# Constants put into the planned order, two output buffers for three, and ten DMA transposes with unused results, in a strided attention and FFN kernel

## Chip, core and metric

The kernel runs on one core of a Trainium2 chip. The metric is the device time of one execution in microseconds (us); the time before is the median of four runs.

## What is computed

The reference takes q, k and v of 8 batches, 8 heads, 576 positions and 64 elements, and five float32 matrices. Heads 0 to 3 attend to the last 32 positions ("local"), heads 4 to 7 to earlier positions with the same remainder modulo 32 ("strided"). The attention output, as 4,608 rows of 512, goes through a multiplicative feed-forward network (FFN):

```
scores = scale * q @ k^T
mask_local   = (rel >= 0) & (rel < 32)
mask_strided = (rel >= 0) & (pos_k % 32 == pos_q % 32)
attn = softmax(where(mask, scores, -1e9)) @ v
x = attn as (4608, 512)
out = ((x @ w1) * (x @ w2)) @ w3 @ w_out
```

## The kernel before, in words

**Stages.** The kernel multiplies w3 and w_out once into one matrix (w34): eight blocks of w3 are transposed on TensorE (`tr`, L552), evicted, and multiplied with w_out (`mm`, L571). Beside that, batch by batch, it does the attention of four pairs of heads (hp 0 and 1 local, 2 and 3 strided): q and k are transposed on TensorE (`T`, L643; the last 64 positions of all heads in one go, `R`, L596), scores (`S`, L686; for batch 0 with a mask bias added by matmuls, L677), exps on ACT (L704), the mask product on DVE (L712), the product with v (`X`, L724 and L734), and the division by the sum, on ACT and DVE (L763 to L790) or on DVE and with a transpose back (L752, L753, `U`, L803). The result is xT, fp16. As soon as the batches of a tile of 512 tokens are done, the FFN of that tile runs, nine tiles in all: for each of eight column blocks jc a product `a` with w1 (L838), its copy asb on ACT, a product `b` with w2 (L854) and the product of both on DVE (L860); then four outputs `o` (L874) of 128 rows each, copied to osb on ACT (L304) and stored by SyncE (L893). A name such as o2_3 is tile 2, output 3; T4_2 is batch 4, pair of heads 2.

**Loads and casts.** All inputs are float32. SyncE loads them through seven staging buffers (`stg`), in the order of the list `_loads`, and POOL casts each to fp16 (L308): q and k of four heads a time (`x16`, two buffers a name), the last positions (`x16r`), v (`v16L`, `v16S`, two buffers by parity of the batch; the columns beyond the 64 elements hold ones, so that the product with v also gives the sums), and the weights.

**What sets the order.** Every step is an operation of a planner (`Plan`): its engines with costs in ns, what it waits for, what it takes and gives back (four PSUM banks "f", two double banks "B", the staging buffers, two asb, three osb, and others), and a rank. `Plan.order` walks through time with those costs and with a rough model of DMA, and picks for each engine the ready operation of lowest rank. It starts each engine at a fixed time (L95: DVE at 6500, ACT at 3200, POOL at 4200), since the constants that stand ahead of the plan occupy it until then. Where TensorE has nothing to do in the first 26 us it inserts a filler matmul (`ps_spin`, L328), which works on zeros. The operations are then issued in the planned order, and each engine executes its own queue strictly in that order. SyncE's queue holds loads and stores alike: a store that waits for its copy, or a load that waits for a staging buffer, holds up all that stands behind it. DMA completions are counted on eight semaphores in rotation, so that a DMA also waits for the one eight before it.

**The constants** stand ahead of the plan (L324 to L387) and are only pinned in part: on POOL the identity, the local mask, `sel` and the causal mask; on DVE zeros for the fillers' weights, kTS, kTL and `place` (L324 to L363), two copies of the identity into `place` (L364, L365), the ones and zeros of v16L and v16S (L382 to L386), the products maskK and maskS and two biases (L373 to L380); on ACT `idR` (L342) and copies of the ones to the second buffers (L385, L387). TensorE makes the strided mask with two small matmuls (L371), which stand at the head of its queue. In the built program DVE does the v16 fills before the two copies into `place`.

**The osb ring.** A copy into osb waits until the store of the copy that used the buffer before has landed.

Of the kernel before, what the change touches and what calls it, by code (L numbers as in the profile page):

```python
# [9 lines left out]
FP32 = mybir.dt.float32  # L10
# [40 lines left out]
class Plan:  # L51
# [34 lines left out]
    def order(self, slack=0, start=None, spin=None, first=("ACT", "DVE", "POOL")):  # L86
# [5 lines left out]
            for d in o.deps:  # L92
                d.succ.append(o)
        free = {k: [(0, i) for i in range(n)] for k, n in self.cap.items()}
        busy = dict(SP=800, POOL=4200, ACT=3200, DVE=6500, PE=1500)  # L95
        busy.update(start or {})
        avail = {e: [] for e in busy}
        for o in ops:
# [158 lines left out]
def kernel(  # L257
# [11 lines left out]
    nc = tc.nc  # L269
# [24 lines left out]

    NSTG = cfg.get("nstg", 8)
    stgs = [consts.tile([P, DF], FP32, name=f"st{i}") for i in range(NSTG)]
    plan = Plan(dict(f=NF, B=2, stg=NSTG, asb=2, osb=3, rcp=2, xqs=2, w3n=3, abt=4))

    def pin(ins):
        return tc.keep_in_program_order(ins)  # L300
# [20 lines left out]

    pin(nc.scalar.preload_act_table_set("natural_log_exp_and_others"))
    w34 = consts.tile([P, KF, DM], FP16)
    nc.vector.memset(w34[:, 0, :], 0.0)  # L324

    def spin(key):
        ps = bank("f", key, [P, DM], FP32)
# [5 lines left out]
    v16L = [consts.tile([P, 4, LT, P], FP16, name=f"v16L{i}") for i in range(2)]  # L333
    v16S = [consts.tile([KB, 4, ST, P], FP16, name=f"v16S{i}") for i in range(2)]
    ptms = [consts.tile([P, 576], FP16, name=f"ptm{i}") for i in range(4)]
    nc.vector.memset(kTS, 0.0)
    nc.vector.memset(kTL[:, :, 0:32], 0.0)
    id16 = consts.tile([P, P], FP16)
    make_identity(nc, id16)

    idR = consts.tile([P, NR], FP16)
    nc.scalar.copy(out=idR.rearrange("p (g u t) -> p g u t", g=4, u=2),  # L342
                   in_=id16[:, 32:32 + NR].rearrange("p (t u g) -> p g u t", u=2, g=4))

    maskL = consts.tile([P, LQ], FP16)
    nc.gpsimd.memset(maskL, 1.0)
# [13 lines left out]
    nc.gpsimd.affine_select(out=causal, in_=causal, compare_op=ALU.is_ge, fill=0.0, base=0,  # L360
                            pattern=[[1, SQ]], channel_multiplier=-1)
    place = consts.tile([SQ, KB], FP16)
    nc.vector.memset(place, 0.0)  # L363
    nc.vector.tensor_copy(out=place[0:64, 32:KB], in_=id16[0:64, 0:64])  # L364
    nc.vector.tensor_copy(out=place[64:SQ, 0:32].rearrange("k (i f) -> k f i", f=4)[:, 0], in_=id16[64:SQ, 64:SQ])  # L365
    maskK = consts.tile([SQ, SQ], FP16)
    maskS = consts.tile([KB, SQ], FP16)
    sel2 = sel.rearrange("r a b -> r (a b)")
    for i, (lhs, rhs, n) in enumerate(((sel2, sel2, SQ), (place, maskK, KB))):
        mps = psp.tile([P, 512], FP32, tag=f"f{i}", name="mps")  # L370
        pin(nc.tensor.matmul(mps[0:n, 0:SQ], lhs, rhs, start=True, stop=True))  # L371
        if i == 0:
            nc.vector.tensor_mul(maskK, mps[0:n, 0:SQ], causal)  # L373
        else:
            nc.vector.tensor_copy(out=maskS, in_=mps[0:n, 0:SQ])

    biasL = consts.tile([P, LQ], FP16)
    biasS = consts.tile([KB, SQ], FP16)
    for o, i in ((biasL, maskL), (biasS, maskS)):
        nc.vector.tensor_scalar(out=o, in0=i, scalar1=-1.0, scalar2=30000.0, op0=ALU.add, op1=ALU.mult)  # L380

    nc.vector.memset(v16L[0][:, :, :, D:P], 1.0)  # L382
    nc.vector.memset(v16L[0][0:32, :, 0, :], 0.0)
    nc.vector.memset(v16S[0][:, :, :, D:P], 1.0)  # L384
    nc.scalar.copy(out=v16L[1][:, :, :, D:P], in_=v16L[0][:, :, :, D:P])  # L385
    nc.vector.memset(v16L[1][0:32, :, 0, 0:D], 0.0)  # L386
    nc.scalar.copy(out=v16S[1][:, :, :, D:P], in_=v16S[0][:, :, :, D:P])  # L387

    xT = [consts.tile([P, NTOK], FP16, name=f"xT{cc}") for cc in range(4)]
    w1h = consts.tile([P, KM, DF], FP16)  # L390
    w2h = consts.tile([P, KM, DF], FP16)
# [20 lines left out]
        o.clean = clean if first else 0  # L412
        return o

    early = []

    def cast(name, key, dmas, eng, fn, deps=(), take=(), last=True, rank=10):
        if eng == POOL and len(early) < cfg.get("early", 0):
            eng = {"POOL": 1040, "DVE": 700, "ACT": 1048}
            early.append(key)  # L420
        return plan.op(name, eng, fn, deps=list(dmas) + list(deps), take=take,
                       give=[("stg", key)] if last else [], rank=rank, lock=True)

    CE = cfg.get("cast", {})
# [38 lines left out]
    def load_qk(b, grp):  # L463
        for nm, ten in (("q", q), ("k", k)):
            key = f"{nm}{b}_{grp}"
            d = dma(key, key, 1530, [P, 4, 4, D],
                    lambda s: s.rearrange("p h c d -> p h (c d)"),
                    ten[b, 4 * grp:4 * grp + 4, 0:NM].rearrange("h (p c) d -> p h (c d)", c=4))

            def fn(e, nm=nm, key=key):  # L470
                t = qkp.tile([P, 4, 4, D], FP16, tag=f"{nm}{grp}", name="x16")
                copy(e, t, stg[key].rearrange("p h c d -> p c h d"))
                x16[(b, nm, grp)] = t

            c = cast("c" + key, key, [d], CE.get("qk", POOL), fn)
            x16op[(b, nm, grp)] = c
            late.append((c, lambda: [Top.get((b - 2, h)) for h in (2 * grp, 2 * grp + 1)]))

    def load_rest(b):
# [19 lines left out]
    def load_vL(b, hp):  # L499
        vt = v16L[b % 2]  # L500
        hs = slice(2 * hp, 2 * hp + 2)
        key = f"vL{b}_{hp}"
        ds = []
        ds.append(dma(key, key, 1500, [P, 2, LT, D], lambda s: s[32:P].rearrange("p h t d -> p (h t) d"),
                      _ap(v, (b * H + 2 * hp) * S * D, [[D, LQ], [LQ * D, 2 * LT], [1, D]]), clean=0))
        cs = []
        for i, pr in enumerate((bass.ds(32, 32), bass.ds(64, 64))):
            def fn(e, pr=pr):
                copy(e, vt[pr, hs, :, 0:D], stg[key][pr])
            c = cast(f"c{key}{i}", key, ds, {"POOL": 825}, fn, last=(i == 1))  # L510
            late.append((c, lambda: [PVop.get((b - 2, h, g)) for h in (0, 1) for g in (0, 1)]))
            cs.append(c)
        hl = plan.op(f"h{key}", cfg.get("halo", {"POOL": 660}),
                     lambda e: copy(e, vt[0:32, hs, 1:LT, 0:D], vt[96:P, hs, 0:LT - 1, 0:D]),
                     deps=cs, rank=9, lock=True)
        late.append((hl, lambda: [PVop.get((b - 2, h, g)) for h in (0, 1) for g in (0, 1)]))
        for g in range(2):
            vop[(b, hp, g)] = cs + [hl]
# [71 lines left out]
    for b in range(B):  # L590
# [28 lines left out]
        for pi, hp in enumerate(cfg["pord"](b)):  # L619
# [51 lines left out]
            def fnS(e, hp=hp, nm2=nm2, w=w, m=m, kT=kT, kw=kw, local=local, pm=pm):  # L671
# [8 lines left out]
                for g in range(2):  # L680
                    sps = bank("B", f"S{nm2}_{g}")
                    for i in range(m):
                        ks, qs = kw * (g * m + i), w * (g * m + i)
                        for h in range(2):
# [2 lines left out]
                                                 qT[r_, hp, qs:qs + w], start=not pm, stop=not pm or i == m - 1))  # L687

            s = Sop[(b, hp)] = plan.op(f"S{nm2}", {"PE": (300 if local else 360) + 500 * pm}, fnS,
                                       deps=evs + Rev + prevPV, take=[("B", f"S{nm2}_0"), ("B", f"S{nm2}_1")],  # L690
                                       rank=rank("S"), soft=True, mode=1)
            for g in range(2):
                sk = f"S{nm2}_{g}"
# [43 lines left out]

                if old:
                    fp = fpo
                pv = PVop[(b, hp, g)] = plan.op(pk, {"PE": 246}, fp, deps=[mo] + vop[(b, hp, g)],  # L740
                                                take=[("B", pk)], rank=rank(f"P{g}"), soft=True)
                ptmu[pslot] = pv
                newPV[g] = pv
# [78 lines left out]
    for t in range(NTILE):  # L822
# [41 lines left out]
        for ts in range(NT // P):  # L864
            parts = 2 if (t == NTILE - 1 and ts == NT // P - 1) else 1
            nw = DM // parts
            for pt in range(parts):
                key = f"o{t}_{ts}_{pt}"
                h = None
                for hf in range(2):  # L870
                    def fo(e, t=t, ts=ts, hf=hf, key=key, pt=pt, nw=nw):
                        ps = bank("f", key, [P, nw], FP32) if hf == 0 else bank("f", key)
                        for ci in range(4 * hf, 4 * hf + 4):
                            pin(nc.tensor.matmul(ps, big[("abt", t)][:, ci, bass.ds(ts * P, P)],  # L874
                                                 w34[:, ci, bass.ds(pt * nw, nw)], start=(ci == 0),
                                                 stop=(ci == KF - 1)))

                    h = plan.op(f"o{t}_{ts}_{pt}_{hf}", {"PE": 864 // parts}, fo,
                                deps=[muls[4 * hf + i] for i in range(4)] + w34op[8 * hf:8 * hf + 8] + [h],
                                take=[("f", key)] if hf == 0 else [], rank=100 + 24 * t + 17 + 2 * ts + 0.001 * hf,  # L880
                                give=[("abt", f"abt{t}")] if ts == 3 and hf == 1 and pt == parts - 1 else [])

                def fc(e, key=key, nw=nw):
                    osb = ffn.tile([P, nw], FP32, tag="osb", bufs=3, name="osb")
                    live[("osb", key)] = osb
                    copy(e, osb, bank("f", key))

                oe = {"ACT": 590 // parts + 60, "DVE": 690 // parts} if parts > 1 else cfg.get("osb", {"ACT": 590})
                c = plan.op(f"osb{key}", oe, fc, deps=[h], take=[("osb", key)], give=[("f", key)], rank=4)

                def fd(e, key=key, t=t, ts=ts, pt=pt, nw=nw):
                    eng = nc.scalar if e == "ACT" else nc.sync
                    pin(eng.dma_start(out_r[t * (NT // P) + ts][:, bass.ds(pt * nw, nw)], live[("osb", key)]))  # L893

                plan.op(f"st{key}", cfg.get("st", {"SP": 450}), fd, deps=[c],
                        give=[("osb", key)], rank=4.5, dma=750 // parts, store=True)
# [42 lines left out]
```

The softmax here doesn't subtract the row's maximum and nothing guards it: scores larger than these inputs give would overflow.

## Time and profile before

| | us |
|---|---|
| runs before | 280.34, 280.70, 281.23, 281.30; median 280.97 |
| the profiled execution's own time | 280.09 |
| span in the profile, first to last instruction | 278.4 |
| PE (TensorE) busy | 266.7 |
| DVE, ACT busy | 174.1, 173.8 |
| POOL busy | 117.9, none of it after 179 us |

The profile counts the time from the first instruction. PE is TensorE's matmuls, PEld its weight loads, SP is SyncE. Bytes moved are 48.65 MB, of them 38.80 MB read from HBM and 9.44 MB written. The granted TensorE clock is 1.0 throughout. In the views a row of the timeline gives start and length in us, engine, line, operation, output<-input, shape and count; in brackets the idle time before it and what ended that.

### The profile page before, as it was taken

The numbers are of one execution on the slowest core, as the hardware profiler recorded it, in microseconds if no ns is written. First come the engines' busy times: TensorE is split into PE (matmuls) and PEld (weight loads), VectorE is DVE, ScalarE is ACT, GpSimd is POOL, SyncE is SP. The second block draws the span as 40 slices with busy tenths as digits, with TensorE's granted clock in tenths as the row PEclk, the third lists the DMA queues.
The fourth block names the chain that finished last, engine by engine and source line by source line (L and its number), as shares of the span: only waits on it lengthen the run. The fifth ranks groups of instructions, "written<-read, shape, count | busy, mean of one in ns | idle before, by whom it ended". The sixth has DMA issues, their size and how long they took to land.

```text
span 278.4 us, 6299 instructions
## 1 busy us (share of the span) xinstructions
PE 266.7 (96%) x2434; PEld 150.8 (54%) x2434; DVE 174.1 (63%) x328; ACT 173.8 (62%) x321; POOL 117.9 (42%) x146
## 2 busy tenths in 40 slices
PE   0989999999999999999999999999999999999995
PEld 0468895746555555555555555555555544444443
DVE  7254677777578667866785778577857763320321
ACT  3562587856667866776588658866885775324321
POOL 6676997599969969450735083100000000000000
PEclk9999999999999999999999999999999999999999
DMA  7999999999999999978365300210030003003004
GB/s 255 322 353 268 355 356 359 259 270 316 298 290 283 338 269 305 264 215 251 105 171 191 122 1 2 114 40 2 1 114 39 2 11 142 1 0 151 2 0 151
DMA packets 53422, 48.65 MB, mean 175 GB/s; under 512 B 20752, under 2 KB 45584, under 8 KB 53392
## 3 DMA queue, kind: packets, MB, share of 16 engines
q1 hardware_dynamic: 53392, 48.24, 57.6%
q8 instruction: 19, 0.31, 0.5%
q14 instruction: 11, 0.09, 0.1%
HBM read 38.80 MB, written 9.44 MB: 173 GB/s over the span
## 4 chain that ended last, share of the span: by engine, by line
PE 95%; DVE 4%; issue 0%; ACT 0%; DVEq 0%
PE ps_o L874 23%; PE ps_b L854 22%; PE ps_a L838 22%; PE ps_T L643 5%; PE ps_mm L571 5%; PE ps_S L686 4%; PE ps_X L734 3%; PE ps_X L724 3%; PE ps_spin L328 2%; PE ps_U L803 2%; PE ps_tr L552 1%; DVE v16S L384 1%; PE ps_R L596 1%; PE ps_S L677 1%; DVE xqs L753 0%; DVE v16L L382 0%
## 5 line engine op out<-in xcount | busy, mean ns | idle before, releaser
L860 DVE TENSOR_TENSOR abt<-ps_b,asb 128x512 f16<-128x512 f32 x72 | 49.4, 689 | 39.3 <-PE ps_b L854 38.7
L838 PE MATMUL ps_a<-xT,w1h 128*128 128x512 f16 x288 | 73.8, 379 | 0.0
L854 PE MATMUL ps_b<-xT,w2h 128*128 128x512 f16 x288 | 73.8, 379 | 0.0
L874 PE MATMUL ps_o<-w,abt 128*128 128x512 f16 (+1 forms) x296 | 67.4, 374 | 0.0
L304 ACT COPY asb<-ps_a 128x512 f32<-128x512 f32 x72 | 42.2, 588 | 40.3 <-PE ps_a L838 39.4
L308 POOL CAST x<-st 128x1024 f16<-128x1024 f32 x32 | 32.7, 1036 | 32.3 <-PE ps_T L643 20.0
L854 PEld LDWEIGHTS <-w2h 128*128 128x128 f16 x288 | 26.9, 98 | 29.2
L874 PEld LDWEIGHTS <-abt 128*128 128x128 f16 x296 | 26.9, 98 | 27.7
L838 PEld LDWEIGHTS <-w1h 128*128 128x128 f16 x288 | 26.5, 98 | 26.6
L704 ACT ACTIVATE ps_S<-ps_S 96x576 f32<-96x576 f32 (+1 forms) x56 | 32.9, 628 | 11.0 <-PE ps_S L686 10.5
L304 ACT COPY osb<-ps_o 128x512 f32<-128x512 f32 x35 | 20.5, 587 | 18.5 <-PE ps_o L874 18.2
L790 DVE TENSOR_TENSOR xT<-ps_X,rcp 64x288 f16<-64x288 f32 x56 | 25.1, 448 | 5.6 <-ACT rcp L774 5.0
L308 POOL CAST v16L<-st 32x768 f16<-32x768 f32 (+1 forms) x32 | 26.3, 821 | 3.1 <-DMA st<-in_v_dram 1.1
L712 DVE TENSOR_TENSOR ptm<-ps_S,maskL 128x576 f16<-128x576 f32 x28 | 19.8, 750 | 12.0 <-ACT ps_S L704 12.0
L753 DVE TENSOR_TENSOR xqs<-ps_X,rcq 96x384 f16<-96x384 f32 (+1 forms) x36 | 20.5, 569 | 1.2
L712 DVE TENSOR_TENSOR ptm<-ps_S,maskS 96x576 f16<-96x576 f32 x28 | 19.8, 749 | 1.3 <-ACT ps_S L704 0.5
L643 PE MATMUL ps_T<-id,x 128*128 128x128 f16 x256 | 19.1, 219 | 0.0
L308 POOL CAST v16S<-st 96x1024 f16<-96x1024 f32 x16 | 16.4, 1033 | 6.3 <-PE ps_X L724 6.3
L774 ACT ACTIVATE rcp<-ps_X 64x576 f32<-64x576 f32 x28 | 18.1, 647 | 0.9
L763 ACT ACTIVATE ps_X<-ps_X 64x576 f32<-64x576 f32 x28 | 17.7, 632 | 0.9 <-PE ps_X L724 0.5
L306 DVE COPY qT<-ps_T 128x512 f16<-128x512 f16 x16 | 11.1, 692 | 9.6 <-PE ps_T L643 8.3
L734 PEld LDWEIGHTS <-ptm 128*96 128x96 f16 (+1 forms) x224 | 14.2, 123 | 4.3
(80 smaller groups left out, 277.0 us busy)
## 6 DMA issues: line engine op xcount, KB each, us to landing
out_dram<-osb SPq DMA_DIRECT2D x35, 256.0 KB
st<-in_moe_w_dram SPq DMA_DIRECT2D x16, 512.0 KB
st<-in_q_dram SPq DMA_DIRECT2D x16, 512.0 KB
st<-in_k_dram SPq DMA_DIRECT2D x16, 512.0 KB
st<-in_v_dram SPq DMA_DIRECT2D x16, 288.0 KB
st<-in_v_dram SPq DMA_DIRECT2D x16, 256.0 KB
st<-in_moe_w_out_dram SPq DMA_DIRECT2D x4, 512.0 KB
st<-in_q_dram SPq DMA_DIRECT2D x8, 128.0 KB
```

Source lines behind the costliest of these rows:

```text
L304: pin(nc.scalar.copy(out=out, in_=in_))
L308: pin(nc.gpsimd.tensor_copy(out=out, in_=in_))
L643: pin(nc.tensor.transpose(ps[:, c * P:(c + 1) * P], x16[(b, x, hp // 2)][:, c, h0:h0 + 2] .rearrange("p h d -> p (h d)"), id16))
L704: pin(nc.scalar.activation(out=sps, in_=sps, func=AF.Exp, bias=0.0, scale=scale))
L712: pin(nc.vector.tensor_mul(ptm[0:kr, 0:576].rearrange("p (h a x) -> p h a x", h=2, x=w), pte[0:kr].rearrange("p h (a x) -> p h a x", x=w), ...
L734: pin(nc.tensor.matmul(xps[0:w, h, i * 65:(i + 1) * 65], ptms[pslot][0:kr, c0:c0 + w], vt[0:kr, 2 * (hp % 2) + h, g * m + i, 0:D + 1], sta ...
L753: pin(nc.vector.tensor_mul(xqs[0:w, 0:m].rearrange("p i h d -> p h i d"), xv[:, :, :, 0:D], _ap(rcp, 0, [[rcp.ap[0][0], w], [4, 2], [1, m] ...
L790: pin(nc.vector.tensor_mul(o, i0, i1))
L838: pin(nc.tensor.matmul(ps, w1h[:, ci, js], xT[ci][:, tok], start=(ci == 0), stop=(ci == KM - 1)))
L854: pin(nc.tensor.matmul(ps, w2h[:, ci, js], xT[ci][:, tok], start=(ci == 0), stop=(ci == KM - 1)))
L860: pin(nc.vector.tensor_mul(big[("abt", t)][:, jc, :], bank("f", f"b{t}_{jc}"), live[("asb", t, jc)]))
L874: pin(nc.tensor.matmul(ps, big[("abt", t)][:, ci, bass.ds(ts * P, P)], w34[:, ci, bass.ds(pt * nw, nw)], start=(ci == 0), stop=(ci == KF - ...
```

## The change

1. **Constants in the plan.** The fills, copies, masks and biases become operations of the planner, pinned in its order. The planner's start times become POOL 3000, ACT 2150, DVE 1300. DVE now does kTS, kTL, `place` and the copies into `place` first, then the masks and biases, then the fills of v16S and v16L; ACT does `idR` first, and the copies of the ones after. The two mask matmuls are planned too: four fillers stand ahead of the first one in TensorE's queue, one between them. A product with v waits for its ones, a score with bias for the biases.
2. **osb has two buffers, not three.** This gives room for 2 KB a partition of a new tile, `junk`. As the planner is told so, it moves output copies back: in tiles 1 to 3 the copies of outputs 2 and 3 stand behind asb copies of the next tile. From tile 1 on TensorE's order changes in places: for example b2_7 stands behind the scores S3_3, and o2_0's second half behind the first half of o2_1.
3. **Ten DMA transposes.** For batches 3 to 7, when the casts of q and k of heads 4 to 7 are done, SyncE issues a DMA transpose of each fp16 tile (128 by 1,024) into `junk`. Nothing reads `junk`. All ten write the same tile, and the built program makes each k transpose wait until the q transpose before it has landed. The planner prices each at 450 ns of SyncE and 1500 ns of DMA. They stand in SyncE's queue between loads and stores: those of batch 3 ahead of the v loads of batch 4, those of batch 4 ahead of the stores of o1_2 and o1_3, those of batch 5 right ahead of the stores of o2_0 and o2_1, those of batch 6 around the v loads of batch 7, those of batch 7 ahead of the store of o4_0.

The list `early`, which was unused (its count is 0), goes away; `on` and `ALT` allow other engines for casts, which the settings don't ask for.

```diff
-        busy = dict(SP=800, POOL=4200, ACT=3200, DVE=6500, PE=1500)
+        busy = dict(SP=800, POOL=3000, ACT=2150, DVE=1300, PE=1500)
...
-    plan = Plan(dict(f=NF, B=2, stg=NSTG, asb=2, osb=3, rcp=2, xqs=2, w3n=3, abt=4))
+    plan = Plan(dict(f=NF, B=2, stg=NSTG, asb=2, osb=2, rcp=2, xqs=2, w3n=3, abt=4))
...
-    nc.vector.memset(kTS, 0.0)
-    nc.vector.memset(kTL[:, :, 0:32], 0.0)
...
-    for i, (lhs, rhs, n) in enumerate(((sel2, sel2, SQ), (place, maskK, KB))):
-        mps = psp.tile([P, 512], FP32, tag=f"f{i}", name="mps")
-        pin(nc.tensor.matmul(mps[0:n, 0:SQ], lhs, rhs, start=True, stop=True))
...
-    nc.vector.memset(v16L[0][:, :, :, D:P], 1.0)
-    nc.vector.memset(v16L[0][0:32, :, 0, :], 0.0)
-    nc.vector.memset(v16S[0][:, :, :, D:P], 1.0)
-    nc.scalar.copy(out=v16L[1][:, :, :, D:P], in_=v16L[0][:, :, :, D:P])
-    nc.vector.memset(v16L[1][0:32, :, 0, 0:D], 0.0)
-    nc.scalar.copy(out=v16S[1][:, :, :, D:P], in_=v16S[0][:, :, :, D:P])
...
+    def first_dve(e):
+        pin(nc.vector.memset(kTS, 0.0))
+        pin(nc.vector.memset(kTL[:, :, 0:32], 0.0))
+        pin(nc.vector.memset(place, 0.0))
+        pin(nc.vector.tensor_copy(out=place[0:64, 32:KB], in_=id16[0:64, 0:64]))
+        pin(nc.vector.tensor_copy(out=place[64:SQ, 0:32].rearrange("k (i f) -> k f i", f=4)[:, 0],
+                                  in_=id16[64:SQ, 64:SQ]))
...
+    pl = plan.op("pool", {"POOL": 0}, lambda e: None)
+    d0 = plan.op("init", {"DVE": 1300}, first_dve)
+    plan.op("idR", {"ACT": 310}, lambda e: pin(
+        nc.scalar.copy(out=idR.rearrange("p (g u t) -> p g u t", g=4, u=2),
+                       in_=id16[:, 32:32 + NR].rearrange("p (t u g) -> p g u t", u=2, g=4))))
+    m0 = plan.op("mk0", {"PE": 100}, mask_mm("mk0", sel2, sel2, SQ), deps=[pl, d0], take=[("f", "mk0")], rank=-200)
+    d1 = plan.op("maskK", {"DVE": 230}, lambda e: pin(
+        nc.vector.tensor_mul(maskK, bank("f", "mk0")[0:SQ, 0:SQ], causal)), deps=[m0], give=[("f", "mk0")])
+    m1 = plan.op("mk1", {"PE": 100}, mask_mm("mk1", place, maskK, KB), deps=[d1], take=[("f", "mk1")], rank=-200)
+    d2 = plan.op("maskS", {"DVE": 230}, lambda e: pin(
+        nc.vector.tensor_copy(out=maskS, in_=bank("f", "mk1")[0:KB, 0:SQ])), deps=[m1], give=[("f", "mk1")])
...
+    for local, c0, c1 in ((False, 1780, 1900), (True, 1620, 1500)):
+        onesop[(0, local)] = plan.op("ones", {"DVE": c0}, lambda e, local=local: ones(e, 0, local), deps=[d2], rank=1)
+        onesop[(1, local)] = plan.op("ones", {"ACT": c1}, lambda e, local=local: ones(e, 1, local),
+                                     deps=[onesop[(0, local)]], rank=8)
...
+    junk = consts.tile([P, 1024], FP16)
...
+            if grp == 1 and b >= 3:
+                plan.op(f"dt{nm}{b}", {"SP": 450}, lambda e, nm=nm: pin(nc.sync.dma_start(
+                    junk.rearrange("p (a b) -> p a b", b=P),
+                    x16[(b, nm, grp)].rearrange("p c h d -> p (c h d)"), transpose=True)), deps=[c], dma=1500, store=True)
...
-                    osb = ffn.tile([P, nw], FP32, tag="osb", bufs=3, name="osb")
+                    osb = ffn.tile([P, nw], FP32, tag="osb", bufs=2, name="osb")
```

## The prediction

> **What bounds the kernel now.** I read the page first (shares, slices, chain), then three stretches, then the timeline of the start, of one tile boundary and of the end.
>
> ```profile
> PE 266.7 (96%) x2434; PEld 150.8 (54%) x2434; DVE 174.1 (63%) x328; ACT 173.8 (62%) x321; POOL 117.9 (42%) x146
> ...
> POOL 6676997599969969450735083100000000000000
> ...
> DMA  7999999999999999978365300210030003003004
> ```
>
> TensorE is the bound; POOL and the DMA engines are full in the first half only. The answer by stretches says where TensorE has a hole (after the stretch: its length, then busy times of PE, PEld, DVE, ACT, POOL, the granted clock, DMA share, GB/s):
>
> ```profile
> 10.00:35.00 25.00, 23.59 (x311) 18.12 (x310) 12.19 (x26) 11.88 (x26) 18.54 (x21) 1.00 1.08 329
> 35.00:140.00 105.00, 105.00 (x1052) 61.41 (x1051) 77.07 (x146) 74.94 (x143) 77.63 (x92) 1.00 0.97 277
> 140.00:275.00 135.00, 135.00 (x1070) 69.99 (x1068) 78.14 (x141) 82.23 (x150) 14.93 (x17) 1.00 0.18 61
> ```
>
> From 35 us to 275 TensorE never pauses. So the end moves only by what happens before about 35 us, by pauses that are new after it, and by the tail after the last matmul. The start (timeline of PE, two rows left out):
>
> ```profile
> 7.28 0.22 PE L371 MATMUL mps<-maskK,place 72*96 72x72 f16 x1 [4.21 <-DVE maskK L373]
> 7.31 3.70 PE L328 MATMUL ps_spin<-w 128*128 128x512 f16 x9
> 10.84 0.61 PE L552 MATMUL ps_tr<-id,w3n 128*128 128x128 f16 x8
> ...
> 11.95 2.75 PE L328 MATMUL ps_spin<-w 128*128 128x512 f16 x12
> 14.54 0.83 PE L643 MATMUL ps_T<-id,x 128*128 128x128 f16 x12
> ```
>
> TensorE's queue stands behind the second mask matmul until 7.28 us, because DVE fills v16L and v16S before the two copies into `place`; the fillers (ps_spin) and the first real transposes come after it. The other end of the start is POOL, whose casts run without a pause from 27.02 to 41.3 us:
>
> ```profile
> 33.27 2.02 POOL L308 CAST w3n<-st 128x1024 f16<-128x1024 f32 x2
> ```
> ```profile
> 34.85 0.43 PE L803 MATMUL ps_U<-id,xqs 96*128 96x96 f16 x6
> 35.12 0.61 PE L552 MATMUL ps_tr<-id,w3n 128*128 128x128 f16 x8
> ```
>
> The first of those two w3 casts ends at 34.30; the transpose that needs it starts at 35.12. That is a slack of 0.8 us, the smallest I found (v16L of batch 0 ends at 30.66 against 31.63; the last w2 cast at 56.93 against 58.61; q, k of batch 2 at 72.34 against 73.98). Last, one tile's output copies and the end:
>
> ```profile
> 122.93 0.58 ACT L304 COPY osb<-ps_o 128x512 f32<-128x512 f32 x1
> 124.20 0.58 ACT L304 COPY osb<-ps_o 128x512 f32<-128x512 f32 x1 [0.68 <-PE ps_o L874]
> 125.30 1.18 ACT L704 ACTIVATE ps_S<-ps_S 128x576 f32<-128x576 f32 x2 [0.52 <-PE ps_S L686]
> 126.39 0.59 ACT L304 COPY osb<-ps_o 128x512 f32<-128x512 f32 x1
> ```
> ```profile
> 273.41 0.58 ACT L304 COPY osb<-ps_o 128x512 f32<-128x512 f32 x1 [1.14 <-PE ps_o L874]
> 274.78 0.86 DVE L306 COPY osb<-ps_o 128x256 f32<-128x256 f32 x2 [5.78 <-PE ps_o L874]
> ```
>
> With three osb buffers each output bank is emptied as soon as its matmuls end.
>
> **What the Trainium skill says.** (1) "DMA: Bandwidth & Descriptors", section "Latency and other measured facts": a DMA transpose moved 261 GB/s on one kernel. No transpose is in the trace of before, so it can't agree or disagree. (2) The same page, "Issuing engines are not separate DMA queues": all DMAs run on the same 16 engines and interleave. The trace agrees: stores and loads share one queue (q1), at 329 GB/s while it is full. (3) "TensorE: Matmul & The Clock Gate", Part 1: an idle array starts at half clock for about 3.4 us. The trace agrees: the first nine fillers take 3.70 us, 0.41 us each, the later twelve about 0.22 us each. So an earlier start of the fillers also warms the array earlier.
>
> **The change part by part.** The sum is made against the profiled execution: span 278.4 us, its own time 280.09 us, which is 0.9 us under the median of 280.97. I add the difference to the median.
>
> *Constants in planned order.* On DVE only kTS (0.72 us), kTL and `place` (0.09 and 0.10 us) and the two copies (0.46 and 0.17 us) now stand ahead of the masks; the v16 fills (1.34 and 1.76 us) go behind them. POOL ends `sel` at 2.75 and `causal` at 2.96 us, so maskK is possible at about 3.2 and the second mask matmul at about 3.5 us instead of 7.28. Fillers start at about 1.3 us. The first w3 transposes then wait for their cast (ends 5.38) and not for the masks: about 5.5 against 10.84 us. The first q, k transposes wait for the k cast that ended at 9.73: about 9.8 against 14.54. That is 4.7 us early, but it does not last. POOL, the loads and SyncE's first 60 DMAs are in the same order, so the casts come when they came: k of the other half ends at 14.91 (lead falls to 17.98 - 14.91 = 3.1), w3 block 3 at 16.88 against 19.50 (2.6), v16L at 30.66 (1.0), the w3 block at 34.30 (0.8). TensorE's order is in sequence, so what is left is **-0.8 us**. Bounds: -1.0 to 0. ACT gets `idR` first and the ones copies (1.90 and 1.47 us) between evictions; cover is the 2.5 us and more that ACT waits for q, k there; nothing.
>
> *Two output buffers for three.* This is two costs. In the tail, the second half copy on DVE needs the buffer of the store issued at 274.02. That store's last packet ends at 275.68 in the trace (1.66 us). The copy started at 275.21 before, so it starts 0.5 us later, and with it the last store: **+0.5 us**.
>
> In tiles 1 to 3 the planner, which sees buffers come free later, has put the third and fourth osb copies behind the next tile's first two asb copies and the exps of the next scores. Until then two of the four PSUM banks stay full. I laid tile 2 to tile 3 out in the new order with the rows of before (matmul group of four 0.86, asb and osb 0.59, exp 0.585, mask 0.71, product 0.69, eviction lag 0.2 us), from b2_7 at 116.7: o2_3 ends at 126.2, T4_2 at 126.9, a3_0 at 127.8. Then b3_0 needs T4_2's bank, which ACT's qT and kTS copies free at 128.35: TensorE waits 0.35 us. b3_0 ends at 129.2, and a3_1 needs its bank, which the product frees at 130.15, while U4_0 was through at 129.85: 0.3 us more. Then the copies of o2_2 and o2_3 come (131.8 to 133.0) and the banks are enough. So 0.65 us a tile, for tiles 1 to 3; in tile 0 the same layout shows no wait, in tiles 4 to 6 the copies move by a place or two, which I take as nothing. **+2.0 us**; bounds 0 (other matmuls fill it) and 6 x 0.65 = 3.9.
>
> *Ten DMA transposes of 256 KB on SyncE.* Their data goes nowhere, so they cost only what queues behind them. The k transpose writes the same junk tile as the q transpose, so SyncE stands until q's has landed; behind it stand the v loads of the next batch and stores. One transpose on an empty queue: issue 1.5 us (rows of SyncE's issues lie between 0.33 and 4.65; my choice) + 256 KB at 261 GB/s 1.0 + what a store has besides issue and movement, 1.66 - 0.33 - 0.7 = 0.6: about **3 us, an estimate**. The first of a pair also waits for about 1 MB of loads ahead in the queue, 3 us at 329 GB/s. A pair so stops SyncE some 7 us. Lower bound: a store's 1.66 us. Upper bound: if every 32-byte piece is a packet of its own, 8,192 packets on 16 engines at 9 ns (4-byte packets of the trace) to 21 ns (256-byte ones) = 4.6 to 10.8 us, so up to 13 us each.
>
> Who waits? The loads behind have room: pair 3 falls at about 85 us in front of v of batch 4, needed at 127. What is tight is tile 2's first store, behind pair 5. By pair 3 (85.4 to 93), pair 4 (104.5 to 111) and v of batch 5, the q cast of pair 5 comes at about 121.5; the pair ends at about 128.5; the store of o2_0 lands at about 130.5. The copy of o2_2 needs that buffer at 131.8. So **0**, with a margin of only 1.3 us. In tiles 3 and 4 the store has 5 us and more.
>
> Sum: -0.8 + 0.5 + 2.0 + 0 = +1.7; 280.97 + 1.7, rounded up for the narrow margin, gives **282.8 us** (own range 281.8 to 285).
>
> **Rivals.** *R1: the transposes are slow and the output ring stops ACT.* At 7.4 us each (4.6 us of packets) every pair before tile 2's store comes 4.4 us later, one on the other: 3 x 4.4 = 13 us, less 1.3 of margin and some 3 us that idle SyncE takes up: ACT stands about 9 us at the copy of o2_2, asb copies stand behind it, TensorE with them: 282.8 + 9 = 292. At 13 us each it is 3 x 10 - 4 = 26 us or more: 309. For it: the margin is thin, no trace shows a transpose. Against: the rate on the skill's page. *R2, not slower: the planner's new order fills the bank waits.* The place is b3_0 and a3_1; it decides if T4_2's eviction ends before 128.0, when ACT takes qT and DVE takes kTS at once. Then -0.8 + 0.5 = -0.3: 280.7. For it: the planner chose this order knowing the banks. Against: ACT's order has qT and kTS in a row. *R3: the lead at the start holds* (casts come earlier because DVE leaves POOL alone), 1.7 us up to the w2 slack and no bank wait: -1.7 + 0.5: 279.8. Against: POOL waited for DMA at 27.02, not for DVE. That the change doesn't do what it says is out: the built order has all ten transposes on SyncE.
>
> **How the numbers follow.** Forecast 0.50; R1 at 292 0.20, its upper end 0.08; R2 0.14; R3 0.08. About 0.3% (0.84 us) is what a measurement of this kernel can tell from no change: faster 0.08 (R3), same 0.14 (R2), slower 0.78. The range 280.2 to 292 leaves out the upper end (0.08), part of R1 (0.06) and part of R3 (0.05).
>
> **What would show it.** Right: second mask matmul at 3.5 us, the w3 transposes of the fifth block at about 34.3; PE waits of 0.3 us at b and a of tiles 2 to 4, released by ACT and DVE; the last DVE copy waiting for a DMA. Wrong: an ACT osb copy that waits microseconds for the out DMA, or SyncE standing 10 us at a transpose (R1); PE without pauses after 35 us (R2).

## The result and the profile after

| | before | after |
|---|---|---|
| median of the runs, us | 280.71 (279.99 to 282.55, 52 runs) | 281.97 (281.21 to 284.70, 33 runs) |
| ratio to before | | 1.0051, 95% interval 1.0039 to 1.0062 |
| the profiled execution's own time, us | 280.09 | 281.97 |
| its span, us | 278.4 | 280.2 |

The change made the kernel slower, by 1.26 us between the medians. The two profiled executions lie 1.88 us apart, because the one of before was a quick one, 0.62 us under its median, and the one of after stands on its median. Differences between the two traces so overstate the loss by some 0.6 us. Medians are over all executions; the ratios leave out three slow ones, two of run 9 and one of run 10, that lay more than 1.5% above the fastest of their kernel.

The page of after, the same lines as of before:

```profile
PE 268.5 (96%) x2433; PEld 150.8 (54%) x2433; DVE 173.2 (62%) x327; ACT 174.2 (62%) x322; POOL 118.3 (42%) x146
...
POOL 6677897699988296493753361100000000000000
...
DMA  7999999999989898997999632210021003003003
```

The busy shares say almost nothing. The stretches say more (columns as in the stretches of before):

```profile
10.00:35.00 25.00, 20.35 (x287) 16.09 (x285) 11.65 (x25) 12.45 (x26) 18.65 (x22) 1.00 1.07 319
35.00:140.00 105.00, 104.80 (x1043) 61.11 (x1041) 76.30 (x145) 74.87 (x143) 77.87 (x91) 1.00 1.02 280
140.00:275.00 135.00, 134.83 (x1066) 69.81 (x1065) 77.81 (x140) 81.95 (x150) 15.36 (x18) 1.00 0.27 79
```

TensorE is no longer unbroken from 35 to 275 us. Only 0.37 us is counted as idle, but the line of milestones below shows more, since the spacing of matmuls that start late also grows without counting as a pause. What TensorE waited for (first columns: who waits <- for whom; then us in all, times, the longest):

```profile
PE ps_tr L580 <- POOL w3n L308: 2.6, 4, 1.2
PE ps_T L671 <- POOL x L308: 1.6, 1, 1.6
...
PE ps_a L866 <- DVE abt L888: 0.2, 1, 0.2
```

The first two rows are the start: TensorE gets to the transposes early and then waits there for POOL's casts. The third is new, a product of the FFN that waits for its PSUM bank. The starts of single matmuls in both traces give the account, in us from the span's start:

| | before | after | difference | step |
|---|---|---|---|---|
| first w3 transpose | 10.84 | 5.42 | -5.42 | |
| fifth w3 block | 28.65 | 28.02 | -0.64 | |
| sixth w3 block | 35.12 | 34.69 | -0.43 | |
| a0_0 and a2_0 | 42.30 and 99.41 | 41.89 and 98.99 | -0.42 | start: -0.42 |
| a3_0 | 126.64 | 126.59 | -0.05 | |
| a5_0 | 181.09 | 182.04 | +0.95 | |
| a7_0 and end of the last matmul | 233.50 and 275.12 | 234.17 and 275.80 | +0.67 | tiles: +1.09 |
| end of the last DVE copy | 275.64 | 277.45 | +1.81 | tail: +1.14 |

(In a3_0 and a5_0, some 0.25 us is order alone: b2_7 and its like stand elsewhere, and at a7_0 that is given back.) The tail, in the timelines of SyncE, ACT and DVE and in the chain that ended last:

```profile
272.11 5.71 SPq L921 DMA_DIRECT2D out_dram<-osb  x5
```
```profile
274.23 0.59 ACT L304 COPY osb<-ps_o 128x512 f32<-128x512 f32 x1 [1.28 <-DMA out_dram<-osb]
```
```profile
275.45 0.42 DVE L306 COPY osb<-ps_o 128x256 f32<-128x256 f32 x1 [5.78 <-PE ps_o L902]
277.03 0.43 DVE L306 COPY osb<-ps_o 128x256 f32<-128x256 f32 x1 [1.15 <-DMA out_dram<-osb]
```
```profile
272.11 2.02 DMA out_dram<-osb
274.84 2.01 DMA out_dram<-osb
```

Before, both DVE halves ran back to back and no store was on the chain. Now the last copy ends 1.65 us after the last matmul in place of 0.52, and two stores, 2.0 us each from issue to release, are on the chain.

### The profile page after: what moved, and what is told of

It reads as the page before. It is cut to its first block, busy times and chain, and to the rows that moved or that the text cites. A ratio compares the mean times of both kernels' runs of the same rounds, so it can differ in the third digit from the quotient of the medians.

```text
span 280.2 us, 6304 instructions
## 1 busy us (share of the span) xinstructions
PE 268.5 (96%) x2433; PEld 150.8 (54%) x2433; DVE 173.2 (62%) x327; ACT 174.2 (62%) x322; POOL 118.3 (42%) x146
## 4 chain that ended last, share of the span: by engine, by line
PE 88%; DMA 7%; POOL 2%; DVE 1%; SPq 1%; ACT 0%; issue 0%; DVEq 0%; ACTq 0%
PE ps_b L882 23%; PE ps_a L866 22%; PE ps_o L902 21%; PE ps_T L671 4%; PE ps_mm L599 4%; PE ps_S L714 4%; DMA st<-in_moe_w_out_dram 3%; PE ps_X L762 3%; PE ps_X L752 3%; DMA st<-in_k_dram 2%; PE ps_U L831 2%; DMA out_dram<-osb 1%; PE ps_tr L580 1%; SPq L311 1%; PE ps_R L624 1%; DVE abt L888 1%
## 5 line engine op out<-in xcount | busy, mean ns | idle before, releaser
L902 PE MATMUL ps_o<-w,abt 128*128 128x512 f16 (+1 forms) x296 | 66.5, 373 | 0.0
L902 PEld LDWEIGHTS <-abt 128*128 128x128 f16 x296 | 27.4, 98 | 28.8
L304 ACT COPY qT<-ps_T 128x512 f16<-128x512 f16 x16 | 9.4, 586 | 12.9 <-PE ps_T L671 12.7
```

Source lines behind the costliest of these rows:

```text
L304: pin(nc.scalar.copy(out=out, in_=in_))
```

## Experiments

My theory was that of the prediction with the sizes of the trace: start gains, the two buffers cost time in the tail and, by the order that comes with them, at PSUM banks in the tiles; the transposes are hidden. Rival A: the transposes are the cost. Rival B: planned constants bring the bad order. Rival C: the start's lead of 5 us holds. Rival D: the transposes' entries in the plan bring the bad order. Each ratio is to executions of the kernel before that were measured beside the run. Where an order is called unchanged, the built programs have the same sequence on TensorE, ACT, DVE and POOL.

**1. No transposes, same order.** The planner still sees the ten entries, but they issue nothing.

```diff
-plan.op(f"dt{nm}{b}", {"SP": 450}, lambda e, nm=nm: pin(nc.sync.dma_start(...)), ...)
+plan.op(f"dt{nm}{b}", {"SP": 450}, lambda e: None, ...)
```

> The ten DMA transposes are left out (their results are unused, so the output is whole), while the planner still sees them: every engine has exactly the order of the changed kernel. My theory: the transposes' own work is hidden on SyncE's queue and in idle DMA time; the time lost lies in the two output buffers and the order that came with them. Then the time stays at 281.9 us (281.6 to 282.2), with the waits of TensorE for a PSUM bank in tiles 3 and 4, and the waits of the last copies for a store, where they were. Rival A, the transposes are the cost (DMA time, or SyncE stopped between the two of a pair, so that stores and loads are late): 280.7 us or below, and the waits in tiles 3 and 4 go.

Measured: 281.61 us, ratio 1.0037 (1.0023 to 1.0051). The tile and tail waits are where they were (a5_0 1.00 us later than before, last DVE copy 1.79). So rival A falls as the main cause.

**2. Constants alone.** The kernel before with the constants planned, three buffers, no transposes and no entries for them.

> The kernel before with only the constants planned and pinned: three output buffers, no transposes, nothing left out. My theory: the start keeps its gain of 0.4 us (first product of tile 0 some 0.4 us earlier than in the kernel before), the tiles and the tail are those of the kernel before: 280.3 us (280.0 to 280.6). Rival B, the planned constants by themselves make the planner choose an order with new waits in the tiles: 281.2 us or more. Rival C, the lead of the first transposes (5 us) holds further than in the full change: 279.8 us or less.

Measured: 279.37 us, ratio 0.9956 (0.9940 to 0.9972). This is faster than both kernels and than I expected: 1.2 us under before (0.8 to 1.7), where I had said 0.4. In the trace everything from a0_0 to the last copy is 0.94 us earlier than in the trace of before, and no new pause comes after it:

```profile
35.00:140.00 105.00, 105.00 (x1054) 61.34 (x1052) 76.90 (x146) 74.94 (x143) 78.38 (x91) 1.00 0.96 276
```

So rival B falls too. The sixth w3 block is 0.94 us earlier than before, so the lead did not hold for its 5 us. By its number (279.8 us or less) rival C was met; but the start differs from that of the changed kernel by no more than executions of one order do: a0_0 stands at 41.37 us here, at 41.89 and 41.75 in two executions of the changed kernel, and at 40.99 in one of run 7.

**3. Two buffers alone.** The kernel before with one number changed.

```diff
-asb=2, osb=3,
+asb=2, osb=2,
...
-tag="osb", bufs=3, name="osb")
+tag="osb", bufs=2, name="osb")
```

> The kernel before with one number changed, two output buffers in place of three, in the plan and the tile. My theory: the last copies wait for stores (+1.1 us, as in the changed kernel), and the planner, which may no longer place two copies to the output ahead of a store, chooses the order with the waits for a PSUM bank (+0.5 us a tile in two to three tiles): 282.4 us (281.8 to 282.8), slower than the changed kernel by the 0.4 us of the start. If the tile waits come from the constants or the transposes and not from the buffers: 281.8 us. Rival A (transposes are the cost): 280.7 us.

Measured: 281.73 us, ratio 1.0039 (1.0024 to 1.0053), so +1.1 us. The trace splits it: the last copy ends 1.60 us after the last matmul, as in the changed kernel, but in the tiles only 0.18 us is lost, once, at b3_0. Here my theory of the tile waits failed: two buffers by themselves don't make them.

**4. Constants and two buffers**, no transposes, no entries for them.

> Planned constants and two output buffers, but no transposes and no entry for them in the plan; nothing left out. The two parts alone gave 279.4 us (constants) and 281.7 us (two buffers). My theory, that the planned entries of the transposes shift the planner's order and bring the waits of tile 4 and of the first product of tile 3, and that the two parts add up: 280.5 us (280.1 to 280.9), with at most 0.2 us lost to PSUM-bank waits. Rival, that constants and two buffers together already make that order: 281.6 us, with the waits of 0.3 us ahead of the second first-product of tiles 3 and 4.

Measured: 280.78 us, ratio 1.0011 (0.9996 to 1.0027). The product of the two parts is 0.9956 x 1.0039 = 0.9995, a hair below the interval; as the two ratios have intervals of their own, the parts add up within what was measured. In the tiles, again 0.18 us at b3_0 only. The ACT timeline ahead of tile 3 shows the difference; first this run, then the changed kernel:

```profile
127.48 0.60 ACT L304 COPY asb<-ps_a 128x512 f32<-128x512 f32 x1
127.96 0.62 ACT L304 COPY osb<-ps_o 128x512 f32<-128x512 f32 x1
129.00 1.18 ACT L727 ACTIVATE ps_S<-ps_S 128x576 f32<-128x576 f32 x2 [0.42 <-ACT osb L304]
130.07 0.61 ACT L304 COPY osb<-ps_o 128x512 f32<-128x512 f32 x1
130.55 0.61 ACT L304 COPY asb<-ps_a 128x512 f32<-128x512 f32 x1
```
```profile
127.75 0.60 ACT L304 COPY asb<-ps_a 128x512 f32<-128x512 f32 x1
129.26 1.18 ACT L732 ACTIVATE ps_S<-ps_S 128x576 f32<-128x576 f32 x2 [0.91 <-ACT asb L304]
130.88 0.59 ACT L304 COPY asb<-ps_a 128x512 f32<-128x512 f32 x1 [0.44 <-PE ps_a L866]
131.36 0.59 ACT L304 COPY osb<-ps_o 128x512 f32<-128x512 f32 x1
132.41 0.59 ACT L304 COPY osb<-ps_o 128x512 f32<-128x512 f32 x1 [0.46 <-DMA out_dram<-osb]
```

Without the entries the two outputs left over from tile 2 are copied at 127.96 and 130.07; with them at 131.36 and 132.41. The two PSUM banks stay full 2 to 3 us longer, and in that time a3_1 runs short (b3_0's wait is there in both).

**5. Three buffers, everything else kept.** The unused target moves into a buffer of the w3 tiles, which is dead by then, so three output buffers and the transposes fit together.

```diff
-junk = consts.tile([P, 1024], FP16)
+big["junk"] = ffn.tile([P, DF], FP16, tag="w3n", bufs=3, name="junk")
...
-osb=2
+osb=3
```

> The changed kernel with three output buffers again, in plan and tile; the transposes stay, and their unused target lies in a buffer of the third-weight tiles, which are dead by then. My theory: the tail's wait goes, the order with the waits in the tiles goes, and the transposes cost nothing: 279.5 us (279.1 to 279.9), as with the constants alone. Rival A, the transposes and the SyncE stops between them cost something whatever the buffers: 280.2 us or more. Rival D, the planned entries of the transposes bring the tile waits whatever the buffers: 280.5 us.

Measured: 279.84 us, ratio 0.9972 (0.9960 to 0.9985). No pause of TensorE over 0.14 us from 100 us on, and the last copy ends 0.52 us after the last matmul. So the entries bring the tile waits only together with two buffers: rival D falls in the form in which I had put it. Two buffers with the entries but without the planned constants were not run.

**6. The same with entries that issue nothing**, order unchanged.

> The run with three output buffers and transposes, with the transposes issuing nothing and the order kept; they are left out, their results are unused. With three buffers a store has one copy more of time before its buffer is needed, so a late store should cost nothing: 279.8 us as with the transposes (279.5 to 280.1). Rival, the transposes cost DMA time that the loads need: 279.3 us or less, 0.5 us under the run with them.

Measured: 279.50 us, ratio 0.9958 (0.9945 to 0.9972). That is the low edge of the range that I had given, above the rival's 279.3, and its interval overlaps that of 5.

**7. The changed kernel and run 1 once more, on one chip.**

> The changed kernel once more, to have it beside the two runs that differ from it in one thing, on one chip: 281.9 us (281.6 to 282.2). What is open: whether the transposes cost nothing (then the empty run below gives the same within 0.2 us) or some 0.4 us (the difference of the medians so far, whose intervals overlap).

> The run that issues no transposes in the changed kernel's order, once more, beside the changed kernel. If the transposes cost nothing: the same time as the run beside it within 0.2 us. If the delay of the stores that they bring costs time in some executions (one profiled execution of the run with the tail buffers lost 0.7 us in tile 4, where ScalarE waited for the store of tile 3's first block): 0.3 to 0.5 us less, with the low ends of both alike and the high end of this one lower.

Measured: 281.84 us, ratio 1.0051 (1.0031 to 1.0071), against 281.64 us, 1.0040 (1.0025 to 1.0055). The high end of the empty run is not lower (284.06 against 283.44). Three comparisons (1, 6, 7) put the transposes at +0.3 to +0.4 us, each with overlapping intervals: one by one they don't exclude zero, though all have the same sign, and 1 us is not in sight. The traces say where such a cost could sit. The first transpose is issued at 84 us, so a0_0 comes too early to be delayed by any. From a0_0 to the end of the last matmul, TensorE takes 233.91 us in both executions of the changed kernel and in both without transposes. Then the last copy ends 1.66 us after the last matmul with them, 1.57 and 1.59 without: under 0.1 us. More than that can only come from executions that these four don't show; run 10 has one.

**8. A second target for k**, order unchanged, so that the second transpose of a pair needn't wait for the first to land.

```diff
-junk = consts.tile([P, 1024], FP16)
+junkq = consts.tile([P, 1024], FP16)
+junkk = ffn.tile([P, DF], FP16, tag="w3n", bufs=3, name="junk")
```

> The changed kernel with a target of its own for the transposes of k, so that the second of a pair no longer waits for the first to land; order and data as in the changed kernel. My theory: SyncE stops at a pair for its two issues alone (2.5 to 4 us in place of 5 to 7), the stores of tiles 2 and 3 go out some 3 us earlier, and the time falls by what the late stores cost: 0 to 0.4 us (281.5 to 281.9). Rival: the first's landing is not what holds the second; the transposes follow one another in the DMA queue anyway, and starts and time stay (281.9).

Measured: 281.89 us, ratio 1.0042 (1.0024 to 1.0060). SyncE's timeline around the pair of batch 5, in the changed kernel and in this run:

```profile
122.23 6.51 SPq L502 DMA_TRANSPOSE junk<-x  x2
128.83 1.01 SPq L921 DMA_DIRECT2D out_dram<-osb  x2
```
```profile
116.73 2.77 SPq L510 DMA_TRANSPOSE junkq<-x  x1
119.60 2.28 SPq L510 DMA_TRANSPOSE junk<-x  x1
122.17 1.11 SPq L929 DMA_DIRECT2D out_dram<-osb  x2
```

The wait for the first's landing does hold SyncE, but it is not all: a pair now takes 3.7 to 5.9 us of SyncE in place of 5.6 to 8.5, more than the 2.5 to 4 that I had expected, since the second issue grows from some 1.2 to 2.3 to 3.1 us. The pair of batch 5 gains 1.4 us; the rest of its lead comes from the pairs before. The store of o2_0 goes out at 122.17 and not at 128.83 us (122.08 in run 1, without any transposes), and still the time is the changed kernel's. So those 6.7 us of delay cost nothing that I can measure.

**9. Each transpose twice**, order unchanged.

```diff
-lambda e, nm=nm: pin(nc.sync.dma_start(...))
+lambda e, nm=nm: [pin(nc.sync.dma_start(...)) for _ in range(2)]
```

> The changed kernel with each transpose issued twice, so 20 in place of 10, in the same place of SyncE's queue, the order of all engines unchanged. Four transposes into one target follow one another, each waits for the one before, so the stop of SyncE at a pair grows from some 5 to 7 us to some 16 us. My theory: the margin of 1.3 us behind the pair of 122 us is used up, the store of tile 2's first block goes out some 9 us later, ScalarE stops at the copy that needs its buffer and TensorE runs out of PSUM banks; the pairs at 103 and 140 us do it too: 288 us or more (288 to 300). Rival: stores and loads have room on the queue, only the time of the DMA engines counts (ten transposes of some 3 us each on 16 shared engines): within 0.5 us of the changed kernel, 281.5 to 282.5 us.

Measured: 309.90 us, ratio 1.0988 (1.0938 to 1.1038), even more than I had said. SyncE, ACT and TensorE around the four of batch 5, and the waits of ACT and TensorE for the whole run:

```profile
136.17 13.61 SPq L502 DMA_TRANSPOSE junk<-x  x4
149.87 1.01 SPq L921 DMA_DIRECT2D out_dram<-osb  x2
```
```profile
152.20 0.59 ACT L304 COPY osb<-ps_o 128x512 f32<-128x512 f32 x1 [11.46 <-DMA out_dram<-osb]
```
```profile
152.83 1.44 PE L882 MATMUL ps_b<-xT,w2h 128*128 128x512 f16 x3 [10.74 <-ACT osb L304]
```
```profile
ACT osb L304 <- DMA out_dram<-osb: 26.1, 7, 11.5
```
```profile
PE ps_b L882 <- ACT osb L304: 16.4, 2, 10.7
PE ps_a L866 <- ACT osb L304: 4.3, 1, 4.3
```

Four transposes hold SyncE for 13.6 us, the store behind them is late, ACT stops 11.5 us at the copy that needs its buffer, and TensorE stops 10.7 us for a bank. This happens in three places (5.7, 10.7 and 4.3 us of TensorE). In each pause the granted clock falls to 0.5, for 6.8, 10.2 and 6.8 us (0.952 over the run), and 13.4 us of these lie behind the pauses, where TensorE works again. At half clock that is a loss of 6.7 us, an estimate; with the 20.7 us of pauses it makes 27.4 of the 27.6 us by which the stretch from a0_0 to the last matmul is longer than in the changed kernel. It is the rival R1 of the prediction, on the far side of its threshold.

**10. Other buffers for the last copies.** In the changed kernel, the copy of o8_2 and the first half of o8_3 go to the two asb buffers, idle by then; order unchanged.

```diff
+XT = (f"o{NTILE - 1}_2_0", f"o{NTILE - 1}_3_0")
...
+if key in XT:
+    osb = ffn.tile([P, NT], FP32, tag="asb", name="osx")[:, 0:nw]
```

> The changed kernel, all of it, with one thing added at the very end: the copies of the last tile's third row block and of the first half of its fourth write to the two buffers of the SwiGLU's first product, which are idle by then, and so wait for no store. The order of every engine is that of the changed kernel. My theory: the 1.28 us wait of ScalarE and the 1.15 us wait of VectorE in the tail go, and the end comes 1.1 us earlier: 280.85 us (280.6 to 281.1), with the last copy ending some 0.5 us after the last product as in the kernel before. Rival: the last store or its queue sets the end whatever the copies do, and the time stays at 281.9 us.

> The run with idle buffers for the last copies once more, since its times spread over 4.4 us (the run with the constants alone: 1.3 us) and its profiled execution stood 0.9 us under its median. My theory: the tail's gain is 1.1 us in every execution, and what spreads is the start and the tiles of this order, as in the changed kernel, whose times spread over 3.5 us: median 280.9 us (280.5 to 281.4), last copy 0.5 us after the last product. Rival: the tail's gain is partly given back elsewhere: 281.4 us or more again, with the last store's landing later.

Measured: 281.42 us, 1.0027 (1.0010 to 1.0044), and again 281.05 us, 1.0028 (1.0010 to 1.0047). In both traces the waits are gone and the last copy ends 0.52 us after the last matmul, so 1.13 us earlier than in the changed kernel. The medians fall by only some 0.65 us. One profiled execution shows a loss that the others don't have, in the timelines of ACT and TensorE in tile 4:

```profile
160.04 1.20 ACT L304 COPY osb<-ps_o 128x512 f32<-128x512 f32 x2 [1.40 <-DMA out_dram<-osb]
```
```profile
160.68 1.02 PE L867 MATMUL ps_a<-xT,w1h 128*128 128x512 f16 x4 [0.54 <-ACT osb L304]
```

The store was issued at 153.00, 0.07 us from its time in the changed kernel, but its last packet ended at 159.53; a packet of 16 KB of the instruction queue ran beside it from 157.31 for 0.98 us. In the changed kernel ACT copied at 158.09; such a packet ran there too, but earlier, from 155.62 to 156.60, and that store's last packet ended at 157.61. How often this happens, and whether it is the rest of the difference between 1.13 and 0.65, stays open.

## Why the prediction was right, and where its sizes were off

The forecast was 282.8 us, from a sum of +1.7 us rounded up; the median is 281.97, +1.26 us and near the low edge of the forecast's own range. Its base of 280.97, from four executions, was 0.26 us above the median of 52. The direction and the places were right. That the sum came so near is in part luck: the tail was 0.6 us too small and the tiles 0.9 us too large, which nearly cancels.

The traces split the loss more sharply than the times do, since the stretch from a0_0 to the end of the last matmul repeats, with one exception, within 0.03 us in executions of one order: 232.82 us before and in run 2, 232.99 in runs 3 and 4, 232.79 and 232.81 in runs 5 and 6, and 233.91 in six of the seven profiled executions of the changed kernel and runs 1, 7, 8 and 10 (234.93 in the other). Run 9 is apart. So in the tiles two buffers cost 0.17 us, the order that comes with the entries 0.92 more, and the transposes nothing. What else spreads from trace to trace lies ahead of a0_0. Term by term:

- *Start, -0.8.* The lead shrank as described, at POOL's casts. In the profiled pair it is -0.42; over twelve profiled executions that share this start, a0_0 lies between 1.31 us before and 1.12 us behind that of before, the middle at -0.5. The times of run 2 give -1.2 (0.8 to 1.7). Both fit if the quick 0.62 us of the trace of before lie at its start: a0_0 would then stand at 42.92 us in a median execution. Run 3 has the same start, and its trace, 0.32 us under its median, gives 42.50 + 0.32 = 42.82. Against 41.89 after, the start is then worth about -1.0, an estimate. What spreads it is the loads: in all fourteen traces the cast of the fifth w3 block starts 0.14 to 0.15 us after its load has landed, at 26.87 us in before, 26.77 in after, and between 25.92 and 28.52 in the others; with the constants planned, a0_0 follows the pair of w3 casts behind it after 8.3 to 8.6 us. So the prediction was right that a DMA held POOL there, though in these two traces the profile's view names PE. Why the loads land when they do was not tried. The failed detail is the assumption that the casts come when they came: the pair of w3 casts began at 33.59 and not 33.27 us, because a load of v landed late (line below; these casts serve the sixth w3 block of the table, which the prediction calls the fifth):

```profile
28.51 1.69 POOL L308 CAST v16L<-st 32x768 f16<-32x768 f32 x2 [0.55 <-DMA st<-in_v_dram]
```

- *Tail, +0.5.* The mechanism was right, the size was 1.14. I had let the copy start when the store's last packet ended (1.66 us after issue, as it was). It started at 277.03, and the last packet ended at 276.50: 0.53 us between them. The store itself was also 0.15 us late, since ACT's copy of o8_2 waited for the store of o8_0. "DMA: Bandwidth & Descriptors" of the Trainium skill, section "Anatomy of one DMA", written for DMAs that GpSimd issues, says that completion, and not setup, dominates the fixed cost of a DMA; it allows about 100 ns for the semaphore after the receipt. Here, with SyncE's stores, it is 0.4 to 0.5 us from the last packet to the waiting engine's start (three cases); no run splits that stretch further.
- *Banks in the tiles, +2.0.* Places right, b and a_1 of tiles 3 and 4. The sum is the mis-sized term: I had 0.65 us a tile for three tiles; measured are 0.21 + 0.32 us for tile 3, 0.21 + 0.29 for tile 4, and 0.12 in place of 0.65 for tile 2, together 1.15. b3_0 started at 127.92, just after the kTS copy ended at 127.87, as laid out. Of these, b3_0's wait comes with two buffers alone (0.18 us in runs 3 and 4). What I had wrong is the cause of the rest: I put the order down to the two buffers. Runs 3 to 5 show that, with the constants planned, it takes two buffers and the transposes' entries in the plan together. That SyncE's planned time pushes back the stores, and so the buffers, is my reading of how the planner works; it was not tried apart. By the times, run 1 against run 4, this order costs 0.7 to 0.8 us, by the traces 0.92.
- *Transposes, 0.* Right within what was measured (+0.3 to +0.4 by the times, zero not excluded; under 0.1 by the traces). The pair of batch 5 came as laid out: stop until about 128.5 predicted, store issued at 128.83 measured. My estimate of 3 us for one holds where nothing runs beside it: in run 9 two of them follow each other on SyncE after 3.06 and 3.10 us (1.23 us of issue, 1.42 of packets, 0.5 to let the next go). At 165.34 in the changed kernel, with a packet of the instruction queue beside it, it took 1.28 us to issue, 2.55 us of packets and 0.65 us to let the next go, 4.4 us in all. The margin was thinner than said: not o2_2's copy but o2_3's waited 0.46 us for a store, without reaching TensorE.

R1 fell for this change but is real: run 9 shows the stop, at twice the number. Its price was too low, as it counted one stop of ACT where run 9 has three, and its 7.4 us for a transpose doesn't follow from its own terms (1.5 + 4.6 + 0.6 = 6.7). R2 fell (the bank waits exist). R3 fell in this form; the start gains more in the times than I had said, and the loss covers it.

What the parts cost, by the times: constants -1.2, two buffers +1.1, the order with the entries +0.7 to +0.8, the transposes +0.3 (not settled): +1.0 together, against +1.4 by the ratio and +1.26 by the medians. The fastest version measured is that of run 2, and run 5 keeps the transposes and is still faster than before: the scarce thing that the change spent was the third output buffer.

## What to carry to other kernels

Price a buffer that you take out of a ring at both ends: in the tail, where nothing covers the wait for a store, a copy now waits for the whole time from a store's issue to its release (2.0 us here, of which 1.1 came on top), and inside, through the order that a planner makes of it. Before you take it, look for a tile that is dead by then. A queue that stood still for 7 us cost nothing measurable here, because the ring behind it had slack; at 14 us it cost 28 us: find the copy that waits for a store and measure how far it is from waiting.

## What the runs showed of the hardware

- A DMA transpose of a 128x1,024 fp16 tile within SBUF moves in 1,024 packets of 256 bytes. With nothing beside it they take 1.42 us (the second of batch 7, at 170.93 in the changed kernel; the same in four other traces and for three transposes of run 9): 262,144 bytes / 1.42 us = 185 GB/s. The 261 GB/s of the Trainium skill's page "DMA: Bandwidth & Descriptors" ("Latency and other measured facts"), on which my estimate rested, was not reached; the measurement decides.
- One 16 KB packet of the instruction queue beside it stretches this. The first transpose of batch 7 took 2.55 us (103 GB/s): such a packet ran from 167.25 to 168.23 us, 937 of the 1,024 packets had started by 167.87, and the other 87 started from 168.21 on. In four other traces the same transpose took 2.6 to 2.9 us, each time with such a packet beside it. Two transposes with separate targets moved together in 3.8 us (139 GB/s), also with such a packet beside them.
- The issue of a transpose holds SyncE for 1.23 to 2.54 us in the changed kernel; a store's took 0.33 to 0.65 in most cases.
- A 16 KB packet of the instruction queue takes about 1 us on its DMA engine (19 of them in the changed kernel, median 1.1).
- In run 9 the granted TensorE clock fell to 0.5 some 2.6 to 4.9 us into each of the three long pauses of TensorE (4.3 to 10.7 us), and came back 3.9 to 5.1 us after its end. The pauses of up to 0.2 us behind a0_0 in the changed kernel did not do it.
